# Attention and two expert layers on one core: two weight loads on another queue, weight blocks four a step, and a conversion moved into the step's own PSUM tile

## The chip, the cores and the metric

The program runs on one core of a Trainium2 chip. The metric is device microseconds of that core, from the program's start to its end. Three runs of the kernel before were timed; their median is 1519.39 us.

## What is computed

The reference is an attention through 32 packed queries per head, followed by two expert layers, one behind the other. Cut to what matters:

```python
p_packed = sm_attn(p, k, v)            # 8 batches x 8 heads, 576 positions, width 64, 32 packed queries
x = sm_attn(q, p_packed, p_packed)     # 4608 tokens x 512
# first layer: w_in 512 x 2048, w_out 2048 x 512
h = x @ w_in
P = a[0] + a[1]*h + a[2]*h*h + a[3]*h*h*h
Q = 1 + abs(b[0])*abs(h) + abs(b[1])*h*h
y = (P / (Q + 1e-06)) @ w_out
# second layer, its own w_in and w_out
h = y @ w_in2
out = (max(h, 0) + alpha * min(h, 0)) @ w_out2
```

The weights arrive as 64-bit floating-point numbers and have to be turned into float32 on the chip, bit by bit.

## The kernel before

**Stages.** The attention runs first, to about 168 us. The first layer is a loop over steps g (the main loop at the end of the loop body, `for g in range(NG + LAG)`): nine chunks of 512 tokens, eight steps each, one step for 256 of the 2048 hidden columns. The second layer follows from about 800 us to the end, on TensorE almost alone.

**One step g.** TensorE multiplies the chunk by the step's columns (`emit_L1`, L588, 24 matmuls into a PSUM tile `h` of two banks; there are two such tiles, so step g + 2 can only start when step g's is free). `emit_E1` and `emit_E2` compute the rational function of h: ScalarE's L677 to L679 (abs, two affine passes), GpSimd's L680, VectorE's L685 and L686, ScalarE's L692 and L693, VectorE's L698 to L700. L693 writes into h, and so has to wait for L686, the last reader of the old values. L700 is the last reader of h. One step later ScalarE (L661) and GpSimd (L662) split the result into a high and a low part, `gt`, and three steps later TensorE multiplies that by w_out (`emit_L2`, L715, 24 matmuls).

**Wb blocks.** The matrix that `emit_L1` uses is not w_in but Wb, the packed values times w_in, so that the last product of the attention need not be written out. Wb is computed in blocks (`emit_Wb`, L446, one block is two matmul records). A block is copied from PSUM by ScalarE (L458, even ones) or VectorE (L456, odd ones) to a tile `wbs` and stored by SyncE (L466). Four PSUM buffers hold such blocks. Of the last sixteen, four stand in `DRAIN`, a hand-written order for the end of the attention, and twelve in the steps that `FILL` names: six in step 0 and six in step 1. At step g the halves of later Wb matrices come back by `fetch_wb` (SyncE, L537) and are split by ScalarE (L546) and GpSimd (L547).

**Late w_out blocks.** Of the sixteen blocks of w_out (128 rows each) the last eight (`LATE`) are loaded and converted in the steps. `load_late` (L597) loads a block of 512 KB. The conversion is: two ScalarE passes, L83 (the magnitude, into a small tile) and L87 (the low bits); then three VectorE passes, `bounded` (L95), `joined` (L98) and `signed` (L101); then a split by ScalarE (L769) and GpSimd (L770). `late_step` places them: L83 and L87 for block s + 1 at the end of step s, L95, L98 and L101 for block s in `emit_E2` ahead of L698, the split of block s at the end of step s + 1. From step 9 on `w2_step` does the same with the second layer's weights.

**What sets the order.** Every engine runs its instructions strictly in the order in which the code emits them, and SyncE issues its DMAs in that order too; nothing is reordered. A DMA waits on its queue for its buffer, and what stands behind it waits with it. The loads L597 of the first two late blocks are emitted by `DRAIN` (the two letters `o`) and stand on SyncE's queue between the stores of Wb blocks.

Of the kernel before, what the change touches and what calls it, by code (L numbers as in the profile page):

```python
# [13 lines left out]
I32 = mybir.dt.int32  # L14
I64 = mybir.dt.int64
U8 = mybir.dt.uint8
AF = mybir.ActivationFunctionType
ALU = mybir.AluOpType
# [10 lines left out]
def attention_then_two_moes(ctx, tc, qT, kT, v, pT, w_in, w_out, ab, w2_in, w2_out, alpha, out):  # L29
    nc = tc.nc  # L30
    mm = nc.tensor.matmul
    act = nc.scalar.activation
    dve = nc.vector
    pool = nc.gpsimd
# [45 lines left out]
    HIGH_R = float(np.array(0x0FEFFFFF, np.int32).view(np.float32))  # L80
# [16 lines left out]
    def joined(wi, low):  # L97
        dve.scalar_tensor_tensor(wi, in0=wi, scalar=3, in1=low, op0=ALU.logical_shift_left, op1=ALU.bitwise_or)  # L98

    def signed(o, wi, high):  # L100
        dve.scalar_tensor_tensor(o, in0=high, scalar=-(1 << 31), in1=wi, op0=ALU.bitwise_and, op1=ALU.bitwise_or)  # L101
# [143 lines left out]
    EARLY = NF // 2  # L245
# [64 lines left out]

    D = 3
    ORDER = "1KVQAWBwwEWwPWwT2WRw"
    FILL = [6, 6]
    DRAIN = "l S1 H A3 B3 E2 W W W W 0 o o A2 B2 E1 A1 B1 o"
    COL = ((0, 0), (1, 1), (0, 1), (1, 0))
    NB = S // 32
# [153 lines left out]
    wb_t, whole_t, wb_q, nwb = {}, {}, [], [0]  # L470
# [83 lines left out]
    w2_st, w2_mag = {}, {}  # L554
# [12 lines left out]
    def w2_bits(n):  # L567

        if w2_st[n].dtype == I64:
            words = w2_st[n].bitcast(I32).rearrange("p (n t) -> p n t", t=2)  # L570
            wi = w2_mag.pop(n).bitcast(I32)
            joined(wi, words[:, :, 0])
            signed(w2_st[n].bitcast(I32)[:, 0:512], wi, words[:, :, 1])
# [5 lines left out]
    def emit_L1(g):  # L579
        c, f = divmod(g, NP)  # L580
        h = psh.tile([128, 2, CH], F32, tag="h", name="h")
        for ft in range(2):
            for v, _, o, m, _ in chunks[c]:
                w = wb_t[v, f]
                n = 0
                for x, y in PASSES:
                    for k in range(2):
                        mm(h[:, ft, o:o + m], w[x][:, k, 128 * ft:128 * ft + 128], a2_t[c][:, y, k, o:o + m],  # L588
                           start=n == 0, stop=n == 5)
                        n += 1  # L590
        hps[g] = h
# [2 lines left out]

    def load_late(n):
        late_st.append(s4_tile(w_out.dtype))
        nc.sync.dma_start(out=late_st[n], in_=w_out[128 * (EARLY + n):128 * (EARLY + n) + 128, :])  # L597

    assert nwb[0] + DRAIN.split().count("W") + sum(FILL) == 8 * B
    for c in DRAIN.split():  # L600
# [65 lines left out]
    def emit_E1(s):  # L666


        late_step(s, "start")
        w2_step(s, "start")  # L670
        if s < NG:
            h = hps.pop(s)
            r_ = spa.tile([128, 2, CH], F32, tag="r_", name="r_", bufs=1)
            q_ = spa.tile([128, 2, CH], F32, tag="q_", name="q_", bufs=2)
            v_ = vs[s] = spa.tile([128, 2, CH], F32, tag="v_", name="v_", bufs=2)
            now[s] = h, r_, q_, v_
            act(r_, h, AF.Abs)  # L677
            act(q_, r_, AF.Identity, scale=b1, bias=b0)
            act(v_, h, AF.Identity, scale=a3, bias=a2c)  # L679
            pool.tensor_tensor(q_, q_, r_, op=ALU.mult)  # L680
        if 1 <= s <= NG:
            emit_hi(s - 1)
        late_step(s, "middle")
        if s < NG:
            dve.tensor_tensor(v_, v_, h, op=ALU.mult)  # L685
            dve.scalar_tensor_tensor(v_, in0=v_, scalar=a1c, in1=h, op0=ALU.add, op1=ALU.mult)  # L686

    def emit_E2(s):

        if s < NG:  # L690
            h, r_, q_, v_ = now.pop(s)
            act(r_, q_, AF.Abs_reciprocal_sqrt, bias=qc)  # L692
            act(h, r_, AF.Square)  # L693
        emit_yo()
        late_step(s, "dve")
        w2_step(s, "dve")
        if s < NG:
            dve.scalar_tensor_tensor(v_, in0=v_, scalar=a0, in1=h, op0=ALU.add, op1=ALU.mult)  # L698
            dve.scalar_tensor_tensor(h, in0=q_, scalar=1.0 + 1e-6, in1=h, op0=ALU.add, op1=ALU.mult)  # L699
            dve.scalar_tensor_tensor(v_, in0=h, scalar=2.0, in1=v_, op0=ALU.subtract, op1=ALU.mult, reverse0=True)  # L700
        late_step(s, "end")
        w2_step(s, "end")

# [50 lines left out]
            nc.sync.dma_start(out=wq_d[y][r // 2][:, 4 * h:4 * h + 4, r % 2, :],  # L754
                              in_=w2_st.pop(n - 1 + h).bitcast(F32).rearrange("p (i f) -> p i f", i=4))

    def late_step(s, part):

        if part == "middle" and s == 0:
            w2_abs(-LATE)  # L760
        elif part == "dve" and s < LATE:
            w2_range(s - LATE)
            w2_bits(s - LATE)
        elif part == "end" and s <= LATE:
            if s:
                i = s - 1
                w = w2_st.pop(i - LATE).bitcast(F32)[:, 0:512]
                t = w_out_t[EARLY + i] = wo_slot(EARLY + i)
                act(t[:, 0, :], w, AF.Copy)  # L769
                pool.tensor_tensor(t[:, 1, :], w, t[:, 0, :], op=ALU.subtract)  # L770
                if s + 2 < LATE:
                    w2_load(s + 2 - LATE)
            if s < LATE - 1:
                w2_abs(s + 1 - LATE)
# [107 lines left out]
    for g in range(NG + LAG):  # L882
        if g == NG:
            close_pool("spx")
            spy = open_pool("spy", bufs=1, side="right")
            load_y(0)
        if g < NG:
            c, f = divmod(g, NP)
            if f == 1 and c + 1 < NCH:
                load_a2(c + 1)  # L890
            if g:
                emit_L1(g)
        if g == LAG - 1:
            close_pool("psw2")
            close_pool("psw")
            psa = open_pool("psa", bufs=1, space=PSUM, side="right")
        emit_E1(g)
        for _ in range(FILL[g] if g < len(FILL) else 0):
            emit_Wb(nwb[0])
            nwb[0] += 1  # L900
        if g < NG and f in (3, 6) and c + 1 < NCH:
            split_a2(c + 1, slice(f // 6, f // 6 + 1))
        w2_step(g, "middle")
        if g >= LAG:
            emit_L2(g - LAG)
        emit_E2(g)
        store_Wb()
        if g < NG:
            next_wb(g)
        d = g - NG  # L910
        if d == -1:
            pool.tensor_scalar(nalpha, alpha_sb, -1.0, None, op0=ALU.mult)
            for n, st in enumerate((gp.tile([128, 2, CH], F32, tag="ast", name="wst", bufs=1),
                                    spa.tile([128, 2, CH], F32, tag="q_", name="wst", bufs=2))):
                for x in range(2):
                    w_load(2 * n + x, st[:, x])
        elif d >= 0:
            if d == 0:
                for n, tag in ((2, "v_"), (3, "q_")):
                    st = spa.tile([128, 2, CH], F32, tag=tag, name="wst", bufs=2)  # L920
                    for x in range(2):
                        w_load(2 * n + x, st[:, x])
            for u in range(4 * d, min(4 * d + 4, SOON)):
                w_split(u, dve)()
            if d:
                split_y(0, d - 1, y_block(0, d - 1, 0))()
# [252 lines left out]
```

## Time and profile before

| | us |
|---|---|
| median of three runs | 1519.39 |
| lowest and highest of them | 1519.29, 1521.09 |
| the profiled execution | 1521.85 |
| its span, first to last instruction | 1519.7 |
| TensorE busy in it | 1459.5 (96%) |
| VectorE busy | 1311.8 (86%) |
| ScalarE busy | 1028.9 (68%) |
| GpSimd busy | 580.3 (38%) |

The engines are PE (TensorE's matmuls; PEld is its weight loads, beside them), DVE (VectorE), ACT (ScalarE), POOL (GpSimd) and SP (SyncE, which issues DMAs; SPq is its queue). The shares are averages over stages with different limits. The granted clock of TensorE has two levels, 1.2 and 2.4 GHz, shown as a mean share of the higher one.

### The profile page before, as it was taken

The numbers are of one execution on the slowest core, as the hardware profiler recorded it, in microseconds if no ns is written. First come the engines' busy times: TensorE is split into PE (matmuls) and PEld (weight loads), VectorE is DVE, ScalarE is ACT, GpSimd is POOL, SyncE is SP. The second block draws the span as 40 slices with busy tenths as digits, with TensorE's granted clock in tenths as the row PEclk, the third lists the DMA queues.
The fourth block names the chain that finished last, engine by engine and source line by source line (L and its number), as shares of the span: only waits on it lengthen the run. The fifth ranks groups of instructions, "written<-read, shape, count | busy, mean of one in ns | idle before, by whom it ended". The sixth has DMA issues, their size and how long they took to land.

```text
span 1519.7 us, 20980 instructions
## 1 busy us (share of the span) xinstructions
PE 1459.5 (96%) x7712; PEld 1207.4 (79%) x7712; DVE 1311.8 (86%) x1416; ACT 1028.9 (68%) x1202; POOL 580.3 (38%) x362
## 2 busy tenths in 40 slices
PE   4799888999999999999999999999999999999998
PEld 2454477888888888888888878888888888888898
DVE  5999799999999999999998899869956996699586
ACT  4456688989898898988886686447434743474363
POOL 3124278788887778887664510000000000000000
PEclk9899999999999999999999999999999999999999
DMA  9999854235443533324436967997567556665694
GB/s 347 318 327 309 285 172 132 70 111 167 162 136 112 201 105 102 114 91 139 142 108 225 336 226 266 381 373 258 207 219 266 193 207 218 239 194 202 217 408 170
DMA packets 150565, 321.20 MB, mean 211 GB/s; under 512 B 14784, under 2 KB 79296, under 8 KB 149440
## 3 DMA queue, kind: packets, MB, share of 16 engines
q1 hardware_dynamic: 147008, 307.29, 58.8%
q0 software_dynamic: 2304, 8.39, 1.4%
q10 hardware_dynamic: 1152, 4.19, 0.8%
q8 instruction: 61, 1.00, 0.3%
q14 instruction: 40, 0.33, 0.1%
HBM read 229.65 MB, written 90.18 MB: 210 GB/s over the span
## 4 chain that ended last, share of the span: by engine, by line
PE 61%; DVE 12%; ACT 10%; issue 3%; POOL 3%; DMA 1%; SPq 0%; ACTq 0%; POOLq 0%; DVEq 0%
PE p L1116 23%; PE p L1108 21%; PE acc L715 10%; PE h L588 6%; DVE s L98 2%; DVE s L101 1%; DVE h L699 1%; PE pw L446 1%; ACT h L693 1%; POOL gt L662 1%; ACT gt L661 1%; DVE v L968 1%; DMA s<-wb_d 1%; DVE s L95 1%; DVE v L951 1%
## 5 line engine op out<-in xcount | busy, mean ns | idle before, releaser
L715 PE MATMUL acc<-gt,wo 128*128 128x512 f32 x1728 | 406.9, 391 | 2.6 <-ACT yo L651 2.6
L715 PEld LDWEIGHTS acc<-gt,wo 128*128 128x128 f32 x1728 | 320.5, 188 | 68.4 <-ACT yo L651 3.8
L1108 PE MATMUL p<-ysp,ws 128*128 128x512 f32 (+1 forms) x1680 | 348.6, 369 | 2.8 <-ACT vsp L1036 2.4
L1116 PE MATMUL p<-vsp,ws 128*128 128x512 f32 (+1 forms) x1680 | 345.8, 368 | 0.0
L1108 PEld LDWEIGHTS p<-ysp,ws 128*128 128x128 f32 x1680 | 293.7, 189 | 57.1 <-ACT vsp L1036 3.4
L1116 PEld LDWEIGHTS p<-vsp,ws 128*128 128x128 f32 x1680 | 292.7, 189 | 52.3
L588 PEld LDWEIGHTS h<-a2t,wb 128*128 128x128 f32 x1728 | 229.9, 192 | 20.6 <-issue 13.9
L588 PE MATMUL h<-a2t,wb 128*128 128x192 f32 (+2 forms) x1728 | 235.1, 293 | 10.9 <-DVE v__1906 L700 4.1
L1036 ACT ACTIVATE vsp<-v 128x1024 fp32r<-128x1024 f32 (+1 forms) x140 | 135.7, 972 | 149.6 <-PE p L1116 100.9
L1037 DVE TENSOR_TENSOR vsp<-v,vsp 128x1024 fp32r<-128x1024 f32 (+1 forms) x140 | 155.8, 1113 | 32.4 <-ACT vsp L1036 31.8
L951 DVE TENSOR_TENSOR v<-v,p 128x1024 f32<-128x1024 f32 (+1 forms) x100 | 110.8, 1110 | 40.6 <-PE p L1108 40.0
L968 DVE SCALAR_TENSOR_TENSOR v<-r,nalpha,v 128x512 f32<-128x512 f32 (+1 forms) x160 | 112.4, 743 | 29.8 <-ACT v L963 29.8
L962 ACT ACTIVATE r<-v 128x1024 f32<-128x1024 f32 (+1 forms) x60 | 58.3, 972 | 76.2 <-DVE v L951 75.9
L951 DVE TENSOR_TENSOR v<-v 128x1024 f32<-128x1024 f32 (+1 forms) x80 | 88.4, 1109 | 0.0
L547 POOL TENSOR_TENSOR wb<-s,wb 128x512 fp32r<-128x512 f32 x48 | 66.3, 1382 | 20.2 <-ACT wb L546 19.7
L95 DVE TENSOR_SCALAR s<-s 128x512 f32<-128x512 f32 x48 | 66.8, 1392 | 0.3 <-ACT s L83 0.3
L963 ACT ACTIVATE v<-v 128x1024 f32<-128x1024 f32 (+1 forms) x60 | 58.6, 976 | 2.0
L446 PE MATMUL pw<-w_in,pph 128*128 128x512 f32 x96 | 51.0, 646 | 6.8 <-ACT wbs L458 6.8
L98 DVE SCALAR_TENSOR_TENSOR s<-s,s 128x512 int32<-128x512 int32 x40 | 56.8, 1420 | 0.3
L976 ACT ACTIVATE v<-p 128x1024 f32<-128x1024 f32 (+1 forms) x20 | 18.8, 942 | 53.2 <-PE p L1108 53.2
L951 DVE TENSOR_TENSOR c<-c,p 128x1024 f32<-128x1024 f32 (+1 forms) x25 | 27.4, 1112 | 30.5 <-PE p L1116 30.3
L381 POOL TENSOR_TENSOR trn<-trn,mx 128x576 f32<-128x576 f32 x16 | 19.2, 1201 | 80.5 <-DVE mx L380 67.8
(1027 smaller groups left out, 2261.4 us busy)
## 6 DMA issues: line engine op xcount, KB each, us to landing
ws<-wh_d SPq DMA_DIRECT2D x224, 512.0 KB, 5.6
wh_d<-ws SPq DMA_DIRECT2D x56, 512.0 KB, 5.0
wq_d<-s SPq DMA_DIRECT2D x32, 512.0 KB, 3.4
wst<-wq_d SPq DMA_DIRECT2D x56, 256.0 KB, 4.0
wb_d<-wbs SPq DMA_DIRECT2D x48, 256.0 KB, 4.8
s<-in_w_out SPq DMA_DIRECT2D x24, 512.0 KB, 4.4
s<-wb_d SPq DMA_DIRECT2D x48, 256.0 KB, 4.3
kt<-in_kT SPq DMA_DIRECT2D x16, 576.0 KB, 6.7
```

The lines of the kernel that those rows point to most:

```text
L95: dve.tensor_scalar(w, w, 0.0, HIGH_R, op0=ALU.max, op1=ALU.min)
L98: dve.scalar_tensor_tensor(wi, in0=wi, scalar=3, in1=low, op0=ALU.logical_shift_left, op1=ALU.bitwise_or)
L446: mm(pw, pph[bp][:, j].rearrange("p a b -> p (a b)"), w_in_t[j, fc], start=True, stop=True)
L547: pool.tensor_tensor(t[:, 1], st, t[:, 0], op=ALU.subtract)
L588: mm(h[:, ft, o:o + m], w[x][:, k, 128 * ft:128 * ft + 128], a2_t[c][:, y, k, o:o + m], start=n == 0, stop=n == 5)
L715: mm(acc[d // 2][:, d % 2, :], w[:, x, 128 * d:128 * d + 128], t[:, y, ft, :], start=f == 0 and (x, y, ft) == (0, 0, 0), stop=f == NP - 1 ...
L951: dve.tensor_tensor(o, a, b, op=op)
L968: dve.scalar_tensor_tensor(v_[:, g], in0=r[:, g], scalar=nalpha[:, f:f + 1], in1=v_[:, g], op0=ALU.mult, op1=ALU.add)
L1036: act(t[:, 0, :, 0:m], src, AF.Copy)
L1037: return lambda: dve.tensor_tensor(t[:, 1, :, 0:m], src, t[:, 0, :, 0:m], op=ALU.subtract)
L1108: mm(ps[:, g, 0:m], w[:, g, x, 128 * k:128 * k + 128], ysp[s, i](z, k), start=not onto and q == 0, stop=q == 5, skip_group_check=again)
L1116: mm(ps[:, d, 0:m], w[:, g, x, 128 * d:128 * d + 128], t[:, z, g, 0:m], start=not onto and n == 0 and g == 0 and q == 0, stop=n == 3 and g ...
```

## The change

Four edits:

1. The first two late loads (n < 2) are issued by GpSimd and not by SyncE.
2. `FILL` is `[4, 4, 4]`: the last twelve Wb blocks stand four each in steps 0, 1 and 2. The closing of their PSUM buffers and the opening of the accumulators' (step 2) moves behind the blocks of step 2.
3. For the late blocks of steps 2 to 7 the three VectorE passes of the conversion stand behind L700 and not ahead of L698.
4. There they keep the intermediate value in the second bank of the step's own h tile, `h[:, 1]`, in PSUM, and not in the small SBUF tile that L83 writes. The first pass reads that tile and writes the bank; the second reads the bank and one word of the raw block and writes the bank; the third reads the other word and the bank and writes the raw block.

```diff
-    FILL = [6, 6]
+    FILL = [4, 4, 4]
...
-        nc.sync.dma_start(out=late_st[n], in_=w_out[128 * (EARLY + n):128 * (EARLY + n) + 128, :])
+        (pool if n < 2 else nc.sync).dma_start(out=late_st[n], in_=w_out[128 * (EARLY + n):128 * (EARLY + n) + 128, :])
...
             dve.scalar_tensor_tensor(v_, in0=h, scalar=2.0, in1=v_, op0=ALU.subtract, op1=ALU.mult, reverse0=True)
+            late_step(s, "free", h)
         late_step(s, "end")
...
-    def late_step(s, part):
+    def late_step(s, part, h=None):
...
-        elif part == "dve" and s < LATE:
+        elif part == "dve" and s < 2:
             w2_range(s - LATE)
             w2_bits(s - LATE)
+        elif part == "free" and 2 <= s < LATE and w_out.dtype == I64:
+            w, raw, high = w2_mag.pop(s - LATE), w2_st[s - LATE], h[:, 1]
+            words, hi = raw.bitcast(I32).rearrange("p (n t) -> p n t", t=2), high.bitcast(I32)
+            dve.tensor_scalar(high, w, 0.0, HIGH_R, op0=ALU.max, op1=ALU.min)
+            joined(hi, words[:, :, 0])
+            signed(raw.bitcast(I32)[:, 0:512], hi, words[:, :, 1])
...
-        if g == LAG - 1:
-            close_pool("psw2")
-            close_pool("psw")
-            psa = open_pool("psa", bufs=1, space=PSUM, side="right")
         emit_E1(g)
         for _ in range(FILL[g] if g < len(FILL) else 0):
             emit_Wb(nwb[0])
             nwb[0] += 1
+        if g == LAG - 1:
+            close_pool("psw2")
+            close_pool("psw")
+            psa = open_pool("psa", bufs=1, space=PSUM, side="right")
```

In the changed file the first of the three passes is L768, and the split L769, L770 is L776, L777.

On VectorE, step 3, the order before is (v is the step's result, h its PSUM tile, s_2020 the small tile, s_1948 the raw block):

```order
L685 TENSOR_TENSOR v__2056<-v__2056,h 128x1024
L686 SCALAR_TENSOR_TENSOR v__2056<-v__2056,coef,h 128x1024
L95 TENSOR_SCALAR s_2020<-s_2020 128x512
L98 SCALAR_TENSOR_TENSOR s_2020<-s_2020,s_1948 128x512
L101 SCALAR_TENSOR_TENSOR s_1948<-s_1948,s_2020 128x512
L698 SCALAR_TENSOR_TENSOR v__2056<-v__2056,coef,h 128x1024
L699 SCALAR_TENSOR_TENSOR h<-q__2055,h 128x1024
L700 SCALAR_TENSOR_TENSOR v__2056<-h,v__2056 128x1024
L685 TENSOR_TENSOR v__2144<-v__2144,h 128x1024
```

and with the change (s_2016 is the small tile, s_1932 the raw block):

```order
L685 TENSOR_TENSOR v__2056<-v__2056,h 128x1024
L686 SCALAR_TENSOR_TENSOR v__2056<-v__2056,coef,h 128x1024
L698 SCALAR_TENSOR_TENSOR v__2056<-v__2056,coef,h 128x1024
L699 SCALAR_TENSOR_TENSOR h<-q__2055,h 128x1024
L700 SCALAR_TENSOR_TENSOR v__2056<-h,v__2056 128x1024
L768 TENSOR_SCALAR h<-s_2016 128x512
L98 SCALAR_TENSOR_TENSOR h<-h,s_1932 128x512
L101 SCALAR_TENSOR_TENSOR s_1932<-s_1932,h 128x512
L685 TENSOR_TENSOR v__2144<-v__2144,h 128x1024
```

The three passes moved from ahead of L698 to between L700 and the next step's L685, and the tile that they write first and second is now h.

On GpSimd, at the end of the attention, the two loads come in ahead of step 0's L680 (trn is a tile of the attention, s_1787 and s_1789 the first two raw blocks):

```order
 L529 TENSOR_TENSOR a2t<-ast,a2t 128x1024
 L381 TENSOR_TENSOR trn<-trn,mx 128x576
+L597 DMA s_1787<-in_w_out 128x512
+L597 DMA s_1789<-in_w_out 128x512
 L680 TENSOR_TENSOR q__1822<-q__1822,r__1821 128x1024
```

They left SyncE's queue, where they stood between the store of a Wb block and two stores of the attention.

On ScalarE, step 0, between the conversion of the first late block and the step's own L692 and L693:

```order
 L83 ACTIVATE s_1828<-s_1787 128x512
 L87 ACTIVATE s_1787<-s_1787 128x512
-L458 ACTIVATE wbs<-pw 128x512 x3
+L458 ACTIVATE wbs<-pw 128x512 x2
 L692 ACTIVATE r__1821<-q__1822,qc 128x1024
 L693 ACTIVATE h<-r__1821 128x1024
```

One copy of a Wb block fewer stands there; the same holds for step 1, and step 2 has two.

## Rows read from the trace of the kernel before

**Rows 1.** Busy us by stretch: start:end, length, engines (instructions), granted clock, DMA share, GB/s

```profile
167.60:201.30 33.70, 23.61 (x98) 15.21 (x97) 27.24 (x36) 25.57 (x33) 12.19 (x7) 0.89 0.75 250
201.30:212.90 11.60, 11.58 (x48) 10.61 (x49) 11.01 (x10) 10.11 (x12) 8.43 (x6) 0.72 0.82 278
212.90:263.20 50.30, 43.75 (x241) 37.32 (x241) 49.64 (x40) 41.43 (x49) 43.03 (x22) 1.00 0.35 115
271.60:1519.70 1248.10, 1238.47 (x6409) 1066.73 (x6407) 1077.96 (x1023) 852.23 (x931) 460.40 (x266) 1.00 0.58 200
```

**Rows 2.** Timeline, one step: start us, us, engine, line, [idle before, what ended it]

```profile
234.78 1.50 DVE L95 TENSOR_SCALAR s<-s 128x512 f32<-128x512 f32 x1
234.95 1.03 ACT L693 ACTIVATE h<-r__2225 128x1024 f32<-128x1024 f32 x1 [0.40 <-DVE v__2227 L686]
...
236.31 0.69 DVE L98 SCALAR_TENSOR_TENSOR s<-s,s 128x512 int32<-128x512 int32 x1
...
237.04 1.68 DVE L101 SCALAR_TENSOR_TENSOR s<-s,s 128x512 int32<-128x512 int32 x1
...
238.09 1.00 ACT L677 ACTIVATE r__2308<-h 128x1024 f32<-128x1024 f32 x1
...
238.63 1.27 DVE L698 SCALAR_TENSOR_TENSOR v__2227<-v__2227,coef,h 128x1024 f32<-128x1024 f32 x1
...
240.28 1.19 ACT L679 ACTIVATE v__2310<-h,coef 128x1024 f32<-128x1024 f32 x1
...
241.08 1.22 DVE L700 SCALAR_TENSOR_TENSOR v__2227<-h,v__2227 128x1024 f32<-128x1024 f32 x1
242.22 1.21 DVE L685 TENSOR_TENSOR v__2310<-v__2310,h 128x1024 f32<-128x1024 f32 x1
...
242.45 3.34 PE L588 MATMUL h<-a2t,wb 128*128 128x192 f32 x24 [1.09 <-DVE v__2227 L700]
...
243.47 1.28 DVE L686 SCALAR_TENSOR_TENSOR v__2310<-v__2310,coef,h 128x1024 f32<-128x1024 f32 x1
243.47 2.41 POOL L662 TENSOR_TENSOR gt<-v__2227,gt 128x1024 fp32r<-128x1024 f32 x1 [0.57 <-ACT gt L661]
```

**Rows 3.** Timeline, from the attention's end to step 9, same columns

```profile
166.66 1.68 POOL L381 TENSOR_TENSOR trn<-trn,mx 128x576 f32<-128x576 f32 x1
...
171.03 1.65 SPq L597 DMA_DIRECT2D s<-in_w_out  x2
171.10 3.59 PE L446 MATMUL pw<-w_in,pph 128*128 128x512 f32 x8
...
173.51 1.19 ACT L679 ACTIVATE v__1823<-h,coef 128x1024 f32<-128x1024 f32 x1
...
176.71 0.66 ACT L83 ACTIVATE s<-s 128x512 f32<-128x512 f32 x1 [2.01 <-DMA s<-in_w_out]
177.18 1.28 DVE L456 COPY wbs<-pw 128x512 f32<-128x512 f32 x2
...
177.82 1.06 ACT L458 ACTIVATE wbs<-pw 128x512 f32<-128x512 f32 x2
...
178.46 3.78 PE L446 MATMUL pw<-w_in,pph 128*128 128x512 f32 x4 [3.76 <-ACT wbs L458]
...
182.88 0.42 DVE L95 TENSOR_SCALAR s<-s 128x512 f32<-128x512 f32 x1
...
186.28 1.02 ACT L677 ACTIVATE r__1904<-h 128x1024 f32<-128x1024 f32 x1 [1.85 <-PE h L588]
...
203.71 1.03 ACT L693 ACTIVATE h<-r__1995 128x1024 f32<-128x1024 f32 x1 [0.41 <-DVE v__1997 L686]
...
263.21 3.09 PE L588 MATMUL h<-a2t,wb 128*128 128x256 f32 x24 [1.35 <-DVE v__2394 L700]
```

**Rows 4.** Eight loads of late blocks (L597), issued by SyncE

```profile
DMA to landing us min/median/max: 3.7/4.4/6.9
```

**Rows 5.** Sixteen loads of w_in in the opening (L137), issued by GpSimd

```profile
DMA to landing us min/median/max: 7.0/9.6/12.7
```

More of the change, by code (lines that the diff above doesn't have):

```diff
@@ L892, in attention_then_two_moes @@
                 emit_L1(g)
+        emit_E1(g)
+        for _ in range(FILL[g] if g < len(FILL) else 0):
+            emit_Wb(nwb[0])
+            nwb[0] += 1
         if g == LAG - 1:
@@ L896, in attention_then_two_moes @@
             psa = open_pool("psa", bufs=1, space=PSUM, side="right")
[L897 to L900, printed above, removed]
         if g < NG and f in (3, 6) and c + 1 < NCH:
```

## The prediction, on record before the result

> **What bounds the kernel now.** I read the busy time by stretch first [rows 1]. From 271.6 us to the end TensorE is busy 1238.47 of 1248.10 us at a granted clock of 1.00. Nothing in the change touches that part: what is gained or lost before it moves the end by the same amount. The time to be had lies in 167.6 to 263.2. In its last 50.3 us (five steps, 10.06 us each) VectorE is busy 49.64 us and TensorE 43.75, so VectorE sets the pace there. In its first 33.7 us no engine is full, TensorE has 23.61 us, and its granted clock is 0.89; in the 11.6 us behind it the clock is 0.72.
>
> The rows of one step show the pace [rows 2]. L95, L98 and L101 (one late w_out block) stand ahead of L698 to L700; L95 and L101 take 1.50 and 1.68 us, L98 0.69. TensorE's L588 waits for L700 to leave the h tile (1.09 us). The fast form is there too: L95 takes 0.42 us in step 0 [rows 3], with no GpSimd pass running. So L95 and L101 lose about a microsecond each beside GpSimd, while L686, with one operand in PSUM, takes 1.28 us beside L662, which runs from the same moment [rows 2]. That pair is the evidence the forecast rests on.
>
> The early rows [rows 3] are read as a chain: loads issued at 171.03, ScalarE's L83 waits 2.01 us for the first and starts at 176.71, L458 behind it at 177.82, and TensorE's fifth Wb block waits 3.76 us for that. Its four matmuls then take 3.78 us where eight took 3.59, which is half speed: the idle stretch also cost the higher of the two clock levels.
>
> **Part one: loads by GpSimd and blocks four a step.** The loads now stand on GpSimd's queue behind L381, which ends at 166.66 + 1.68 = 168.34, instead of behind SyncE's stores at 171.03 [rows 3]. GpSimd's next instruction, L680 of step 0, needs ScalarE's L678, which runs just ahead of L679 (173.51), so the two issues have some 5 us and delay nobody. Landing takes 3.7 to 6.9 us for this source from SyncE [rows 4], 7.0 to 12.7 for GpSimd's loads in the opening [rows 5]. I take 6.3, inside the first row, because the opening is the crowded part of the kernel; both ends stay for the range. The first load lands at 174.7. ScalarE wants it when L679 ends, 173.51 + 1.19 = 174.70, so the 2.01 us wait goes.
>
> Replayed with the rows' durations: L83 at 174.75; L458 follows 1.11 later as now (176.71 to 177.82) and takes 1.06 for two blocks, not three, to 176.9; L692 and L693, each near the 1.03 us of L693 [rows 2], end at 179.1; the next L83 and L87 take 1.11 again, so L677 of step 1 can start at 180.2. It starts at 186.28 now, behind a 1.85 us wait for TensorE [rows 3]. That wait goes too: with four blocks TensorE is through at 171.10 + 3.59 = 174.7 and goes straight on to L588, without the 3.76 us idle and the slow clock. VectorE: its two L456 end at 178.46, the conversion takes 0.42 + 0.69 + 0.69 [rows 2, 3] to 180.3, and L698 to the end of L700 takes 241.08 + 1.22 - 238.63 = 3.67 [rows 2], to 183.9.
>
> Step 1: L677 to the end of L679 takes 241.47 - 238.09 = 3.38, to 183.6. L661 waits for L700 (183.9) and takes about 1.05, two L458 1.06, L692 1.1, so L693 starts at 187.2, after VectorE's L686 (186.5). From L693's start to the next L677 it is 238.09 - 234.95 = 3.14, so L677 of step 2 starts at 190.3 and its L679 ends at 193.7. VectorE meanwhile: L685 and L686 to 186.5, two L456 to 187.8, conversion to 189.6, L700 ends 193.3. Then L661, two L458 and L692 put L693 of step 2 at 197.0. Now it starts at 203.71 [rows 3]: **6.7 us earlier**. The blocks moved to step 2 add two L458 there, counted, and two L456, which lie ahead of L698 while VectorE waits for L693. TensorE waits about 2 us for h in each of steps 1 and 2, before L588. If the clock falls there, L588 takes 3 us more, which ScalarE, on other work, does not see.
>
> **Part two: conversion in the h tile.** Six conversions (steps 2 to 7) leave their place ahead of L698 and stand behind L700; the second h bank holds the intermediate. Each instruction then has one SBUF operand. The trace has no integer pass into PSUM. Nearest rows: L98 at 0.69 undisturbed, L95 at 0.42 undisturbed, and 1.50 and 1.68 disturbed [rows 2, 3]. L456, with one PSUM operand like all three, takes 1.28 for two. I take the pitch from L98 to L101, 0.73, for all: 2.15 in place of 3.87 in the step shown. GpSimd's passes lose their disturbance as well; they are off the chain.
>
> The Trainium skill (VectorE: DVE Perf Modes, Why PSUM operands drop a tier) has a rule that a PSUM operand keeps a 32-bit pass at the plain rate; by it the first instruction takes 0.69, as I have it, and by the 0.42 of step 0 the whole would come to 1505.5 us.
>
> New loop, from L693's start: L693 1.03, then L698 to L700 and on to the next instruction 2.45 + 1.14 (238.63 to 241.08 to 242.22), conversion 2.15, with 0.05 of hand-over: 6.82 until VectorE takes L685. ScalarE's side gives L679's end at 241.47 - 234.95 = 6.52, so VectorE is later, by 0.3. Then L685 to L686 1.25, L686 1.28, 0.05: **9.40 us a step** (9.15 if ScalarE were the later). TensorE needs 43.75 / 5 = 8.75 [rows 1], so it fits, though h is now released only at the end of the conversion. What is late next is thus ScalarE and VectorE in turn.
>
> From L693 of step 2 to TensorE's L588 of step 9, which waits for the last h tile concerned, it is 263.21 - 203.71 = 59.50 now [rows 3]; then 5 x 9.40 + 6.87 = 53.9: **5.6 us less**. The SyncE queue: in the new order the fetch of a wb half waits for GpSimd's L547 of the same step. L546 stands just ahead of L677, so 3 us behind L693's start; L547 has half the elements of L662's 2.41 and ends about 1.5 later; the fetch is wanted at the next L546, 9.40 behind the last, so it has some 7.4 us. The longest landing of a load of twice its size is 6.9 [rows 4], so I cost it at nothing.
>
> **Sum.** 6.7 + 5.6 = 12.3 us. The profiled execution took 1521.85 us with a span of 1519.70; the median of the three runs is 1519.39, and I take the sum off that: **1507.1 us**.
>
> **Rivals.**
> *The GpSimd loads land late.* With the usual 9.6 of [rows 5] L83 starts at 178.0, 3.2 later, and ScalarE, which leads the whole chain of part one, gives 3.2 back: 1510.3; with 12.7 it is 1513.4. For it: the only GpSimd loads in the trace. Against: they ran in the crowded opening, and VectorE now has short passes. In the Trainium skill (SBUF — State Buffer, Who interferes with whom) there is a rule that speaks against the change: descriptors of a GpSimd DMA are starved while VectorE runs its two-port passes; by it the loads would come at the late end, at up to 1513.4.
>
> *Slower: VectorE is held in the conversion as before.* If the passes with one PSUM operand wait for GpSimd after all, each at 1.50, 1.68 and 1.68 [rows 2], a conversion takes 4.86 and holds h and L685: 2.71 more, six times, 16.3, against a gain of 12.3: 1523.4. It decides from 12.3 / 6 = 2.05 more, a conversion of 4.2 us. Against it stands L686 beside L662 at 1.28 [rows 2].
>
> *TensorE is the bound.* If conversions fell wholly into VectorE's gaps, steps would take 8.75: 59.50 - 5 x 8.75 - 6.87 = 8.9 in part two, 1503.8. Against: both other paths are longer, 9.15 and 9.40.
>
> *Given back.* If a later wait (the shifted w_in loads, the wb fetches) eats the lead, the time is about 1519. Against: TensorE at 1238 of 1248 us leaves little room [rows 1].
>
> **How the numbers follow.** Forecast 0.66 (1505 to 1509.5), late loads 0.14, TensorE 0.05, given back 0.08, slower 0.07 (0.05 by the price above, 0.02 for a cause not seen). A measurement of this kernel can tell about 0.2% (3 us) from no change: faster 0.66 + 0.14 + 0.05 = 0.85, same 0.08, slower 0.07. The range 1504 to 1512 takes in the forecast, most of the late loads and the edge of the TensorE case, some 0.8.
>
> **What would show it.** L83 of step 0 at 174.7 to 175.5 without a wait; no TensorE gap near 175 and full clock there; L693 of step 2 near 197; the three instructions behind L700 at 0.65 to 0.75 each with GpSimd beside them; L693 to L693 9.4 in steps 3 to 7; L588 of step 9 near 250.6 and TensorE full from there. Wrong if L83 still waits, if the conversion takes over 3 us, or if TensorE waits anew behind 260.

## The result, and the profile after

The changed kernel takes 1507.83 us (median of five runs, 1507.35 to 1508.56) against 1521.09 us for the kernel before, timed with it (five runs, 1519.29 to 1522.55): a ratio of 0.9915, with a 95% interval of 0.9902 to 0.9929. Against the median that the forecast was made from, 1519.39, it is 11.6 us less. The profiled execution took 1507.35 us, with a span of 1505.6.

Between the two profiled executions the span differs by 14.1 us. Not all of that is the change: L381, the last GpSimd instruction of the attention, starts at 165.10 us after and at 166.66 before [rows 3], and nothing ahead of it was touched. That 1.56 us is how the two executions differ in the attention, and it is taken off in all that follows: times of a trace are counted from the start of this L381, or shifted by 1.56 to stand beside those of before.

First the busy time by stretch of the kernel after (start:end, length, then PE, PEld, DVE, ACT and POOL busy with instructions, granted clock, DMA share, GB/s):

```profile
166.10:196.20 30.10, 25.05 (x122) 18.42 (x121) 28.45 (x38) 28.25 (x36) 16.67 (x10) 0.94 0.86 290
191.50:194.50 3.00, 3.00 (x12) 3.00 (x13) 2.45 (x3) 3.00 (x5) 3.00 (x2) 0.50 0.96 355
196.20:249.20 53.00, 49.39 (x266) 41.73 (x264) 46.22 (x47) 49.13 (x59) 44.17 (x26) 1.00 0.47 156
257.50:1505.60 1248.10, 1238.48 (x6410) 1066.86 (x6409) 1078.09 (x1023) 852.85 (x931) 460.04 (x266) 1.00 0.58 200
```

The last row answers to the last of [rows 1]: over the same length, up to the end, TensorE is busy 1238.48 us, before 1238.47, at full clock. It begins 0.29 us ahead of the L588 of step 10 (257.79); from that L588 to the end it is 1247.8 us, and before it was 1248.1 (271.62 to 1519.70). So all of the gain but 0.3 us lies ahead of that L588, and none is given back behind it. In the third row VectorE is busy 46.22 of 53.00 us, no longer all of the time; TensorE with 49.39 and ScalarE with 49.13 now stand ahead of it, and none is full.

Then the timeline of the attention's end and the first steps, with the columns of [rows 3]:

```profile
165.10 1.67 POOL L381 TENSOR_TENSOR trn<-trn,mx 128x576 f32<-128x576 f32 x1
...
166.72 1.14 POOL L597 DMA_DIRECT2D s<-in_w_out  x2
...
169.54 3.59 PE L446 MATMUL pw<-w_in,pph 128*128 128x512 f32 x8
...
171.94 1.19 ACT L679 ACTIVATE v__1823<-h,coef 128x1024 f32<-128x1024 f32 x1
...
172.12 2.40 POOL L680 TENSOR_TENSOR q__1822<-q__1822,r__1821 128x1024 f32<-128x1024 f32 x1 [4.26 <-ACT q__1822 L678]
...
172.57 3.67 PE L588 MATMUL h<-a2t,wb 128*128 128x192 f32 x24
...
173.03 0.67 ACT L83 ACTIVATE s<-s 128x512 f32<-128x512 f32 x1
...
176.81 0.42 DVE L95 TENSOR_SCALAR s<-s 128x512 f32<-128x512 f32 x1
...
178.43 1.00 ACT L677 ACTIVATE r__1895<-h 128x1024 f32<-128x1024 f32 x1
...
182.47 3.33 PE L588 MATMUL h<-a2t,wb 128*128 128x192 f32 x24 [2.80 <-DVE v__1823 L700]
...
191.49 4.89 PE L588 MATMUL h<-a2t,wb 128*128 128x192 f32 x24 [2.26 <-DVE v__1897 L700]
...
194.97 1.03 ACT L693 ACTIVATE h<-r__1972 128x1024 f32<-128x1024 f32 x1
```

The two loads are issued right behind L381 and delay nobody: L680 behind them waits 4.26 us for L678. L83 of step 0 starts at 173.03 behind L679 (171.94 + 1.19) without a wait, L588 follows the four blocks of L446 without a gap, and L693 of step 2 starts at 194.97. What TensorE waits for now is h: 2.80 us and 2.26 us in steps 1 and 2. Behind the second of these its L588 took 4.89 us; the row of the stretch 191.50 to 194.50 above shows the clock granted there, 0.50, the lower of the two levels.

Last the timeline of one step, same columns, to be held against [rows 2]:

```profile
213.91 1.03 ACT L693 ACTIVATE h<-r__2142 128x1024 f32<-128x1024 f32 x1 [0.32 <-DVE v__2144 L686]
...
217.42 1.22 DVE L700 SCALAR_TENSOR_TENSOR v__2144<-h,v__2144 128x1024 f32<-128x1024 f32 x1
...
218.68 0.69 DVE L768 TENSOR_SCALAR h<-s 128x512 f32<-128x512 f32 x1
...
219.41 0.70 DVE L98 SCALAR_TENSOR_TENSOR h<-h,s 128x512 int32<-128x512 int32 x1
219.47 2.39 POOL L680 TENSOR_TENSOR q__2226<-q__2226,r__2225 128x1024 f32<-128x1024 f32 x1 [0.97 <-ACT q__2226 L678]
220.14 0.69 DVE L101 SCALAR_TENSOR_TENSOR s<-s,h 128x512 int32<-128x512 int32 x1
...
220.75 1.21 DVE L685 TENSOR_TENSOR v__2227<-v__2227,h 128x1024 f32<-128x1024 f32 x1
...
220.98 3.34 PE L588 MATMUL h<-a2t,wb 128*128 128x192 f32 x24 [0.66 <-DVE s L101]
...
223.38 1.03 ACT L693 ACTIVATE h<-r__2225 128x1024 f32<-128x1024 f32 x1 [0.34 <-DVE v__2227 L686]
```

L768, L98 and L101 take 0.69, 0.70 and 0.69 us, and 2.07 us pass from L768's start to L685's. L98 starts 0.06 us ahead of GpSimd's L680 and runs on beside it, and L101 lies wholly inside it; L768 is over before it begins. (Step 7, shown further down, has L768 inside L680 as well.) L588 now waits for L101 and not for L700. From L693 to L693 it is 9.47 us.

### The profile page after: what moved, and what is told of

It reads as the page before. It is cut to its first block, busy times and chain, and to the rows that moved or that the text cites. A ratio compares the mean times of both kernels' runs of the same rounds, so it can differ in the third digit from the quotient of the medians.

```text
span 1505.6 us, 20984 instructions
## 1 busy us (share of the span) xinstructions
PE 1451.6 (96%) x7712; PEld 1202.6 (80%) x7712; DVE 1298.3 (86%) x1416; ACT 1028.6 (68%) x1202; POOL 577.2 (38%) x364
## 4 chain that ended last, share of the span: by engine, by line
PE 53%; DVE 15%; ACT 13%; issue 3%; POOL 3%; DMA 1%; SPq 0%; ACTq 0%; POOLq 0%; DVEq 0%
PE p L1123 23%; PE p L1115 21%; PE acc L716 6%; PE h L588 3%; DVE h L699 2%; DVE s L98 2%; ACT h L693 2%; ACT gt L661 1%; DVE s L101 1%; POOL gt L662 1%; ACT s L83 1%; DVE v L975 1%; DVE v L958 1%; DMA s<-wb_d 1%; ACT s L87 1%
## 5 line engine op out<-in xcount | busy, mean ns | idle before, releaser
L588 PEld LDWEIGHTS h<-a2t,wb 128*128 128x128 f32 x1728 | 227.7, 191 | 19.1 <-issue 7.6
L588 PE MATMUL h<-a2t,wb 128*128 128x192 f32 (+2 forms) x1728 | 232.3, 291 | 9.1 <-DVE s L101 3.8
L95 DVE TENSOR_SCALAR s<-s 128x512 f32<-128x512 f32 x42 | 57.6, 1370 | 0.5 <-ACT s L83 0.5
L98 DVE SCALAR_TENSOR_TENSOR s<-s,s 128x512 int32<-128x512 int32 x34 | 50.7, 1491 | 0.1
L446 PE MATMUL pw<-w_in,pph 128*128 128x512 f32 x96 | 48.0, 617 | 1.5 <-ACT wbs L458 1.5
L381 POOL TENSOR_TENSOR trn<-trn,mx 128x576 f32<-128x576 f32 x16 | 19.2, 1198 | 78.5 <-DVE mx L380 59.4
```

## The experiments

The kernel before itself had medians from 1518.99 to 1521.09 us in the four comparisons, so each run is given against the kernel before on its own chip, with the interval of the ratio. The last column is free of that and of the attention's variation: in the profile of each, the time from L381 to the L588 of step 10, from which TensorE is nearly without a gap, less the same time of before, 271.62 - 166.66 = 104.96 (271.62 is the start of that L588 in the trace before, where the last stretch of [rows 1] begins). One trace stands behind each number of that column, and it leaves out what lies behind that L588, 1245.8 to 1248.5 us in these profiles.

| kernel | median us | before, same chip | ratio, 95% interval | trace, against before |
|---|---|---|---|---|
| the changed kernel | 1507.83 | 1521.09 | 0.9902 to 0.9929 | -12.3 |
| the same, once more | 1507.52 | 1518.99 | 0.9908 to 0.9935 | -12.3 |
| part one alone | 1511.74 | 1519.82 | 0.9933 to 0.9963 | -8.1 |
| loads alone | 1516.12 | 1518.99 | 0.9974 to 0.9991 | -2.7 |
| blocks alone | 1514.99 | 1518.99 | 0.9955 to 0.9980 | -6.1 |
| part two alone | 1515.41 | 1519.82 | 0.9959 to 0.9981 | -5.2 |
| new place, SBUF tile | 1520.31 | 1519.82 | 0.9994 to 1.0012 | -1.2 |
| three passes more | 1520.74 | 1519.82 | 0.9997 to 1.0016 | +0.8 |
| first pass in SBUF | 1511.68 | 1518.99 | 0.9936 to 0.9961 | -7.8 |
| first pass in SBUF, steps 2 to 6 | 1507.21 | 1519.55 | 0.9903 to 0.9930 | -12.9 |
| first pass ahead of L698 | 1507.02 | 1519.55 | 0.9903 to 0.9930 | -13.5 |
| all loads by GpSimd | 1511.76 | 1519.55 | 0.9933 to 0.9960 | -9.2 |

### Part one alone, part two alone

Part one alone is the changed kernel without the new place:

```diff
-        elif part == "dve" and s < 2:
+        elif part == "dve" and s < LATE:
...
-            late_step(s, "free", h)
```

> Only part one: GpSimd issues the first two late loads, FILL is [4, 4, 4]; the conversion stands ahead of L698 in the small SBUF tile as in the kernel before. Theory (two independent terms in a row): 7.0 us less than the kernel before (6.7 forecast, 7.2 between the traces), near 1514; L693 of step 2 starts near 195 to 197, the steps behind it stay near 10.0 us. Rival (part one pays only with the conversion out of step 2's way): less than 4 us gained.

Measured 8.1 us less, 1.1 more than expected. L381 starts at 166.30 and L693 of step 2 at 196.15, which is 29.85 us where before it was 37.05: the 7.2 us of the changed kernel's trace. The two steps behind it take 20.6 us (196.1 to 216.7) where before they took 21.4 (203.7 to 225.1), which is nearly all of the rest. The conversion of step 4 in its timeline shows the old form as in [rows 2]:

```profile
216.52 1.48 DVE L95 TENSOR_SCALAR s<-s 128x512 f32<-128x512 f32 x1
...
218.76 1.67 DVE L101 SCALAR_TENSOR_TENSOR s<-s,s 128x512 int32<-128x512 int32 x1
```

Part two alone has `FILL = [6, 6]`, the loads on SyncE and the pools closed where they were before:

```diff
-    FILL = [4, 4, 4]
+    FILL = [6, 6]
...
-        (pool if n < 2 else nc.sync).dma_start(out=late_st[n], in_=w_out[128 * (EARLY + n):128 * (EARLY + n) + 128, :])
+        nc.sync.dma_start(out=late_st[n], in_=w_out[128 * (EARLY + n):128 * (EARLY + n) + 128, :])
```

> Only part two: the conversions of steps 2 to 7 behind L700 with the intermediate in h; loads by SyncE, FILL [6, 6]. Theory: L83 of step 0 waits some 2 us for its load and TensorE some 3.8 us as before, the steps are 9.46 us from L693 to L693, and 5.1 to 5.6 us are gained: near 1515.5. Rival (the second part lives on the lead of the first): less than 3 us gained.

Measured 4.4 us less by the medians (2.9 to 6.2 by the interval), 5.2 in the trace. L693 of steps 3 to 8 starts at 211.9, 221.3, 230.8, 240.3, 249.7 and 259.2, so its steps are 9.46 us. Its timeline shows both of the old waits in step 0:

```profile
175.58 0.66 ACT L83 ACTIVATE s<-s 128x512 f32<-128x512 f32 x1 [2.12 <-DMA s<-in_w_out]
...
177.33 1.98 PE L446 MATMUL pw<-w_in,pph 128*128 128x512 f32 x4 [3.86 <-ACT wbs L458]
```

The rivals fall in both: neither part needs the other. The sum of the two alone is 12.5 us by the medians and 13.3 in the traces, against 12.3 in the trace of both together, so at most about 1 us is gained twice.

Half of that 1 us is no effect of the change. Up to L693 of step 2, part two alone runs the same code as the kernel before, and it gets there 36.55 us behind L381 (165.44 to 201.99), where the kernel before took 37.05. One difference between the two is in the fences: the four matmuls of L446 took 1.98 us here, at a granted clock of 1.00 (177.33 to 179.30), and 3.78 us before [rows 3], at 0.50 (178.46 to 181.20).

### The two halves of part one

The kernel before with the loads on GpSimd and nothing else, and the kernel before with `FILL = [4, 4, 4]` and the pools closed behind the blocks of step 2 and nothing else:

```diff
-        nc.sync.dma_start(out=late_st[n], in_=w_out[128 * (EARLY + n):128 * (EARLY + n) + 128, :])
+        (pool if n < 2 else nc.sync).dma_start(out=late_st[n], in_=w_out[128 * (EARLY + n):128 * (EARLY + n) + 128, :])
```

```diff
-    FILL = [6, 6]
+    FILL = [4, 4, 4]
```

> The kernel before with one edit: the first two late loads issued by GpSimd; FILL [6, 6], the conversion as before. Theory (the two halves of part one remove two waits that lie one behind the other on ScalarE's chain): L83 of step 0 starts right behind L679, 2.0 us sooner, all behind it 2.0 us sooner, near 2 us less than the kernel before; TensorE still waits near 1.8 to 3.8 us for its fifth block. Rival (the fifth block's wait absorbs it): under 0.7 us.

> The kernel before with one edit: FILL [4, 4, 4] and the pools closed behind the blocks of step 2; loads by SyncE, the conversion as before. Theory: TensorE goes from the fourth block straight to L588, L83 of step 0 still waits 2 us for its load, and 5.2 us (4.5 to 6) of part one's 7.2 to 8.1 are gained. Rival (the load is the last wait, and the blocks alone move nothing): under 2 us.

Timeline of the first, loads alone, in step 0:

```profile
173.85 0.67 ACT L83 ACTIVATE s<-s 128x512 f32<-128x512 f32 x1
...
175.60 1.13 PE L446 MATMUL pw<-w_in,pph 128*128 128x512 f32 x2 [1.66 <-ACT wbs L458]
```

L83's wait is gone, and TensorE's fifth block still waits, now 1.66 us. Timeline of the second, blocks alone:

```profile
173.82 3.67 PE L588 MATMUL h<-a2t,wb 128*128 128x192 f32 x24
...
176.54 0.69 ACT L83 ACTIVATE s<-s 128x512 f32<-128x512 f32 x1 [2.16 <-DMA s<-in_w_out]
```

Here L588 starts straight behind the blocks, at 173.82, while L83 waits its 2.16 us. The loads gave 2.9 us by the medians and 2.7 in the trace, where 2.0 was expected; the blocks gave 4.0 by the medians (3.0 to 6.8 by the interval) and 6.1 in the trace, where 5.2 was expected. Together that is 6.9 to 8.8, about the 8.1 of part one: the two waits are separate, as the theory had it, and the rivals, by which one would hide the other, fall. Why both gave 0.7 to 0.9 us more in the trace than expected is not shown; the 0.5 us told above may be a part of it.

### The place or the PSUM tile

The changed kernel with the new place, but the intermediate in the small SBUF tile:

```diff
-            w, raw, high = w2_mag.pop(s - LATE), w2_st[s - LATE], h[:, 1]
+            w, raw, high = (lambda m: (m, w2_st[s - LATE], m))(w2_mag.pop(s - LATE))
```

> The changed kernel, but the intermediate of the six moved conversions stays in the small SBUF tile; place and order as changed. h is then released at L700, some 2.1 us sooner. Theory (the PSUM operand is what spares the pass its wait for GpSimd): the three passes take near 1.5, 0.7 and 1.7 where GpSimd runs beside them, 3.9 in place of 2.1, so steps near 11 us and 10 us slower than the changed kernel, near 1518. Rival (the place alone makes the gain): passes of 0.4 to 0.7, steps at or below 9.46 us, 1506 to 1508.

Its steps are 11.15 us (L693 at 206.2, 217.3, 228.5, 239.6 and 250.8), and the time is that of the kernel before: all of part one's gain is gone. The timeline of one conversion:

```profile
222.00 0.42 DVE L768 TENSOR_SCALAR s<-s 128x512 f32<-128x512 f32 x1
...
222.45 0.70 DVE L98 SCALAR_TENSOR_TENSOR s<-s,s 128x512 int32<-128x512 int32 x1
...
222.89 2.50 POOL L680 TENSOR_TENSOR q__2226<-q__2226,r__2225 128x1024 f32<-128x1024 f32 x1 [0.98 <-ACT q__2226 L678]
223.18 2.76 DVE L101 SCALAR_TENSOR_TENSOR s<-s,s 128x512 int32<-128x512 int32 x1
```

The conversion still takes 3.9 us, as the theory said, but not as 1.5, 0.7 and 1.7: the first two passes are over or under way when GpSimd's L680 starts, and the third waits for all of L680 and ends 0.55 us behind it. So the place alone gains nothing, it costs: 6.9 us in the traces against part one alone, which has the same tile in the old place. The PSUM operand is what makes the difference to the changed kernel, 11.1 us in the traces.

### A conversion made longer

The changed kernel with the first pass issued four times:

```diff
-            dve.tensor_scalar(high, w, 0.0, HIGH_R, op0=ALU.max, op1=ALU.min)
+            for _ in range(4):
+                dve.tensor_scalar(high, w, 0.0, HIGH_R, op0=ALU.max, op1=ALU.min)
```

> The changed kernel with the first conversion pass (L768) issued four times in a row in each of the six moved conversions: 3 x 0.69 = 2.07 us more a conversion. Theory (VectorE and ScalarE's hand-over sets the step, nothing has slack behind it): each step 2.07 us longer, 12.4 us in six, near 1520, equal to the kernel before within 2 us, which is the point that the prediction named (4.2 us a conversion). Rival (TensorE's 8.75 us or ScalarE sets the step and VectorE has slack): under 9 us more, 1516 or less.

The four passes of step 3 in its timeline, and TensorE's wait for the conversion over steps 4 to 9 (waited for: us in total, times, longest), first of this kernel:

```profile
212.32 2.88 DVE L769 TENSOR_SCALAR h<-s 128x512 f32<-128x512 f32 x4
```

```profile
PE h L588 <- DVE s L101: 13.9, 6, 3.1
```

and the same line of the changed kernel:

```profile
PE h L588 <- DVE s L101: 3.8, 6, 0.9
```

Steps are 11.65 us (L693 from 207.5 to 265.8, five steps), 2.18 more than 9.47, and six times 2.18 is the 13.1 us by which it is slower than the changed kernel in the traces. Nothing behind the conversion has slack: each microsecond added to it costs six. The price per pass was the pitch, 0.73, and not the 0.69 of one pass, which the expectation used.

### The first pass back in SBUF

The first pass writes the small tile again, where it takes 0.42 us undisturbed; the second reads that tile and a word of the raw block and writes h:

```diff
-            dve.tensor_scalar(high, w, 0.0, HIGH_R, op0=ALU.max, op1=ALU.min)
-            joined(hi, words[:, :, 0])
+            bounded(w)
+            dve.scalar_tensor_tensor(hi, in0=w.bitcast(I32), scalar=3, in1=words[:, :, 0], op0=ALU.logical_shift_left, op1=ALU.bitwise_or)
```

> The changed kernel, but of the six moved conversions the first pass stays in the small SBUF tile (0.42 us undisturbed); the second reads it and one word of the raw block, both in SBUF, and writes h in PSUM; the third as changed. It ends 0.2 us before GpSimd's L680 starts in the trace of the changed kernel. Theory (a pass with one PSUM operand, read or written, does not wait for GpSimd; VectorE is the later by 0.3 us): 0.42 + 0.70 + 0.69, steps 9.2 in place of 9.46, 1.2 to 1.7 us less than the changed kernel. Rival (what spares the wait is that only one operand is read from SBUF): the second pass takes near 2.5 us beside L680, steps near 11 us, 8 us or more slower.

4.2 us slower than the changed kernel (1511.68 against 1507.52 on the same chip), and neither theory had that. In the timeline, steps 4 and 7 (L769 is the new second pass):

```profile
217.98 0.42 DVE L95 TENSOR_SCALAR s<-s 128x512 f32<-128x512 f32 x1
...
218.43 0.70 DVE L769 SCALAR_TENSOR_TENSOR h<-s,s 128x512 int32<-128x512 int32 x1
...
218.88 2.50 POOL L680 TENSOR_TENSOR q__2226<-q__2226,r__2225 128x1024 f32<-128x1024 f32 x1 [0.96 <-ACT q__2226 L678]
...
245.74 2.38 POOL L680 TENSOR_TENSOR q__2470<-q__2470,r__2469 128x1024 f32<-128x1024 f32 x1 [0.21 <-ACT q__2470 L678]
245.96 2.44 DVE L95 TENSOR_SCALAR s<-s 128x512 f32<-128x512 f32 x1
...
248.07 2.54 POOL L662 TENSOR_TENSOR gt<-v__2394,gt 128x1024 fp32r<-128x1024 f32 x1
...
248.44 2.73 DVE L769 SCALAR_TENSOR_TENSOR h<-s,s 128x512 int32<-128x512 int32 x1
```

In steps 2 to 6 both passes are over, or under way, when L680 starts, and steps take 9.3 us. Behind L693 of step 7 there is no L83 and no L87 left on ScalarE, so the next L680 starts earlier, and then L95 waits for the end of L680 and L769 for the end of L662: 2.44 and 2.73 us. From L693 of step 7 to that of step 8 it is 13.14 us, 3.7 more than in the changed kernel (9.46). The next L588 waits 4.76 us for L101 and then takes 4.61 us, where in the changed kernel it took 3.09. The changed kernel in the same step:

```profile
246.74 2.40 POOL L680 TENSOR_TENSOR q__2470<-q__2470,r__2469 128x1024 f32<-128x1024 f32 x1 [0.23 <-ACT q__2470 L678]
...
247.08 0.69 DVE L768 TENSOR_SCALAR h<-s 128x512 f32<-128x512 f32 x1
...
247.81 0.70 DVE L98 SCALAR_TENSOR_TENSOR h<-h,s 128x512 int32<-128x512 int32 x1
```

L768 and L98 run at 0.69 and 0.70 us in the middle of L680. So the theory was too wide: it is not enough that one operand is in PSUM. L769 writes to PSUM and waits, since it reads two operands from SBUF; L98 and L101 of the changed kernel read one. The Trainium skill (SBUF — State Buffer, Who interferes with whom) states this rule: a VectorE instruction with two SBUF inputs contends with a GpSimd instruction that reads SBUF, one with at most one such input, outside the two-port modes, does not. L769's 2.73 us against L98's 0.70 agree with it.

With the change in steps 2 to 6 alone, step 7 as in the changed kernel:

```diff
+            if s < LATE - 1:
+                bounded(w)
+                dve.scalar_tensor_tensor(hi, in0=w.bitcast(I32), scalar=3, in1=words[:, :, 0], op0=ALU.logical_shift_left, op1=ALU.bitwise_or)
+            else:
+                dve.tensor_scalar(high, w, 0.0, HIGH_R, op0=ALU.max, op1=ALU.min)
+                joined(hi, words[:, :, 0])
```

> The changed kernel with the first pass of the conversion kept in the small SBUF tile in steps 2 to 6, as in the run before, and in step 7 as changed, since in step 7 GpSimd's L680 comes earlier and the second pass, which reads two SBUF operands, took 2.73 us beside L662 there. Theory (that one step was all of the loss): steps 9.3 in place of 9.46, 0.7 us less than the changed kernel, 1506.8 within 1 us. Rival (the form itself costs 4 us): 1511 or more.

1507.21 us, and 0.6 less than the changed kernel in the traces: that one step was all of the loss.

### The first pass where VectorE waits

As the last, with `bounded(w)` of steps 2 to 6 ahead of L698, in VectorE's 1.16 us wait for L693:

```diff
+        elif part == "dve" and s < LATE - 1:
+            w2_range(s - LATE)
```

> As the last, but in steps 2 to 6 the first pass stands ahead of L698, where VectorE waits 1.16 us for L693 with GpSimd's L662 running; the two others behind L700, the second reading the small tile and writing h; step 7 as changed. Theory (a pass on SBUF alone ends just behind the GpSimd pass that it meets): the first pass takes 0.8 to 1.0 us and delays L698 by some 0.3, the conversion behind L700 takes 1.4 and ends before L680 has gone far, steps 9.1 to 9.2, 1.0 to 1.8 us less than the changed kernel, near 1506. Rival (the second pass now meets L680 or the first delays GpSimd): its 2.5 us, steps of 10 us and more, 3 us or more slower.

The timeline of step 4 (L771 is the second pass):

```profile
213.63 2.41 POOL L662 TENSOR_TENSOR gt<-v__2056,gt 128x1024 fp32r<-128x1024 f32 x1
...
214.68 1.65 DVE L95 TENSOR_SCALAR s<-s 128x512 f32<-128x512 f32 x1
...
219.95 0.70 DVE L771 SCALAR_TENSOR_TENSOR h<-s,s 128x512 int32<-128x512 int32 x1
...
220.46 2.43 POOL L680 TENSOR_TENSOR q__2226<-q__2226,r__2225 128x1024 f32<-128x1024 f32 x1 [0.95 <-ACT q__2226 L678]
```

L95 meets L662, waits for its end (1.65 us, where 0.8 to 1.0 was expected) and delays L698 by 0.3 us, L771 is over when L680 has run for 0.2 us, and steps take 9.21 us (196.5 to 242.6 in five) in place of 9.46. That is 1.2 us less in the trace, against the changed kernel, and the medians say 1507.02 against 1507.52 and 1507.83: the lowest time of all, but no measurement here tells it from the changed kernel.

### All loads by GpSimd

```diff
-        (pool if n < 2 else nc.sync).dma_start(out=late_st[n], in_=w_out[128 * (EARLY + n):128 * (EARLY + n) + 128, :])
+        pool.dma_start(out=late_st[n], in_=w_out[128 * (EARLY + n):128 * (EARLY + n) + 128, :])
```

> The changed kernel with all eight late loads issued by GpSimd and not only the first two. The six that move are issued in the steps, beside VectorE's passes. Theory (landing of a GpSimd load here is set by the other traffic): 3.5 to 7 us to landing, as the two of the changed kernel, and no time lost, since such a block has most of two steps before it is read: 1507.5 within 2 us. Rival (the prediction's late-landing case: GpSimd's loads are held up by VectorE's passes): 7 to 12.7 us to landing; the time would still move by less than 3 us.

The landing of the eight loads:

```profile
DMA to landing us min/median/max: 3.6/5.0/7.0
```

No load was late, and yet the kernel is slower than the changed one, by 3.1 us in the traces and some 4 by the medians. The timeline of step 0 shows why:

```profile
175.83 0.53 POOL L597 DMA_DIRECT2D s<-in_w_out  x1 [7.34 <-ACT wbs L458]
...
176.38 2.37 POOL L680 TENSOR_TENSOR q__1822<-q__1822,r__1821 128x1024 f32<-128x1024 f32 x1
...
178.78 1.15 ACT L692 ACTIVATE r__1821<-q__1822,qc 128x1024 f32<-128x1024 f32 x1 [2.91 <-POOL q__1822 L680]
```

The third load waits 7.34 us on GpSimd's queue for its buffer, and L680 of step 0 stands behind it: it starts at 176.38, which is 10.65 us behind L381 (165.73). In the changed kernel it starts as soon as L678 is done, at 172.12, which is 7.02 us behind L381. ScalarE's L692 waits 2.91 us for it, and L693 of step 0 is 3.0 us later behind L381 than in the changed kernel, so the loss is there already. The row names ScalarE's L458 as what freed the buffer; in the kernel before the same load left at 175.13, ahead of that L458 (177.82), so something else is likelier. In the code the buffer had held a Wb block, and the landing of that block's store would fit, but no run shows it. So the theory was right on the landing, the rival was not, and neither had the time: what a load by GpSimd costs here is what stands behind it on the queue while it waits. The changed kernel moves just the two loads whose buffers are free.

## Why the prediction was right

**Sum and terms.** 12.3 us were forecast, and 12.3 is the difference of the traces from L381 on (84.28 us to the L588 of step 9, where before it was 96.55). Part one was forecast at 6.7 and came to 7.2; part two at 5.6 and came to 5.1. That the two errors cancel in the sum is luck. So is part of how near the time came: the 12.3 us were taken off 1519.39, while the kernel before had a median of 1521.09 beside the changed one and 1518.99 beside its repetition, which makes the gain 13.3 and 11.5 us by the medians.

| step of the replay | forecast | trace after, shifted by 1.56 |
|---|---|---|
| L83 of step 0 | 174.75 | 174.59 |
| L677 of step 1 | 180.2 | 179.99 |
| L693 of step 1 | 187.2 | 187.02 |
| L677 of step 2 | 190.3 | 190.15 |
| L693 of step 2 | 197.0 | 196.53 |
| conversion | 2.15 | 2.07 |
| one step | 9.40 | 9.46 to 9.47 |
| L693 of step 2 to L588 of step 9 | 53.9 | 54.41 |

**Part one.** Each of the first four points is 0.15 to 0.2 us early, from the hand-overs at the beginning; the fifth adds 0.3, in the stretch between L679 and L693 of step 2. That L83's wait and the fifth block's are two separate ones is shown by the two halves alone. The excess of 7.2 over 6.7 is no more than the variation of the base: against the 36.55 us that part two alone took up to L693 of step 2, with the code of before, it would be 36.55 - 29.87 = 6.7. The prediction also laid the slow clock of the fifth block's four matmuls to the wait ahead of them; part two alone had a longer wait there (3.86 us) and no slow clock, so the wait by itself does not explain it. The landing was taken at 6.3 us; the first load took 5.9 and the second 6.6, and L83 starts without a wait 6.3 us behind the first issue (166.72 to 173.03). All eight loads of the changed kernel:

```profile
DMA to landing us min/median/max: 3.5/4.1/6.6
```

**Part two.** The pair on which it rested, L686 beside L662, was the right evidence: the passes went at 0.69 and 0.70 beside GpSimd, L98 and L101 in every step and L768 in step 7. The reason was put too widely there, as one operand in PSUM, and as one SBUF operand each, where L101 reads one and writes another. The first pass in SBUF showed what counts for a pass that has an operand or its result in PSUM: the number of operands that it reads from SBUF. In the changed kernel each reads one. What was 0.5 us too small is the length of the stretch: 0.06 in each of five steps, most of it between L685 and L693 (2.63 us for 2.58), and 0.2 in the tail, from L693 of step 7 to L588 of step 9 (7.07 for 6.87). The first pass takes 0.69, as the Trainium skill's rule has it that the prediction cites (VectorE: DVE Perf Modes, Why PSUM operands drop a tier), and not the 0.42 by which the sum would have been 1505.5.

**The cover.** The wb fetch was costed at nothing: in the changed kernel's trace from 170 to 260 us no ScalarE instruction waits for a DMA. The late h cost TensorE 3.8 us over six steps; no ScalarE instruction waited for a matmul there, as forecast. The clock fell behind h in step 2, where L588 took 4.89 us, 1.6 more than the 3.34 of [rows 2]. In three of the variants, with the same code up to there, it fell in step 1 instead and L588 took 6.10 us, near the 3 us more that the prediction named (first pass ahead of L698, first pass in SBUF in steps 2 to 6, new place with the SBUF tile). L693 of step 2 came 29.87 us behind L381 in the changed kernel and 29.96 to 29.97 in these three, so ScalarE hardly saw it, as forecast.

**The rivals.** *Late loads*: no; with all eight on GpSimd, six of them issued beside VectorE's passes, they landed in 3.6 to 7.0 us. The Trainium skill's rule of starved descriptors (SBUF — State Buffer, Who interferes with whom) is neither borne out nor refuted by that: hardly a VectorE pass in those stretches was of the undisturbed 0.42 us form. *Slower*: with the SBUF tile a conversion took 3.9 us in the new place and the kernel was equal to the one before, and with 2.2 us more in PSUM likewise; the point named, 4.2 us a conversion, lies right there. *TensorE the bound*: 9.46 a step against 8.75, and a step of 9.21 was still to be had. *Given back*: from the L588 of step 10 to the end it is 1247.8 us, before 1248.1, and TensorE does not wait anew.

## What to carry to other kernels

Where a VectorE pass runs beside GpSimd, count the operands that it reads from SBUF: with one, and the destination or the other operand in PSUM, it kept its 0.7 us; with two it waited for the end of the GpSimd instruction, up to 2.1 us more, wherever it wrote. With one, and the result in SBUF too, it waited as well: L95 took 2.44 us where L768, the same pass into PSUM, took 0.69. A PSUM tile that the step has just done with is a place for such an intermediate, at the price that the tile's next writer waits for the end of it. A load on a compute engine's queue is free only as long as its buffer is: here two loads gained 2.9 us, and where a third stood behind them and waited 7.3 us for its buffer, about as much was lost again (3.1 us in the traces, some 4 by the medians).

## What the runs showed that was not expected

- The attention ahead of the change varied by up to 1.9 us from one profiled execution to the next (the last L381 started between 164.73 and 166.66 us in the thirteen profiles), more than several of the effects that were looked for; a trace difference says something only from an anchor behind it.
- The clock did not fall behind every wait of TensorE, and not each time behind the same one. Behind 2.8 us of waiting in step 1, with the same code up to there, L588 took 3.33 us in the changed kernel (granted clock 1.00) and 6.10 with the first pass ahead of L698 (0.50). Behind the 2.26 us of step 2 it took 4.89 in the changed kernel. Where it falls was not settled.
- A VectorE pass with SBUF operands alone does not slow down beside GpSimd, it waits: L95 took 0.42 us with no GpSimd pass running, 2.44 us when L680 had just begun, and 1.65 us when L662 was under way for 1.05 us; it ended 0.3 us behind the GpSimd pass both times.
